# Regrouping TensorE's small-tile work, and a gate on VectorE, in a DiT block

## The chip, the cores and the metric

One core of one Trainium2 chip. The metric is the device time of one execution in microseconds (us). Whole times come from repeated executions; a profile is one execution. All whole times compared here are of runs recorded as fast.

Names: PE is TensorE's matmul stream, PEld its weight loads, DVE VectorE, ACT ScalarE, POOL GpSimd, SP SyncE, which starts the weight transfers. ACTq is ScalarE's instruction queue, here when it starts a transfer.

## The reference

A diffusion-transformer block, B = 2 batches of N = 256 tokens, D = 1152, F = 4608, H = 2 heads of Dh = 576.

```python
mod = (silu(c) @ w_mod).reshape(B, 6, 1, D)
shift_a, scale_a, gate_a, shift_m, scale_m, gate_m = [mod[:, i] for i in range(6)]
h = layernorm(x) * (1 + scale_a) + shift_a
q, k, v = split(h @ wqkv)                        # (B, N, H, Dh) each
attn = softmax(q @ k.T * Dh ** -0.5)             # per batch and head
x = x + gate_a * ((attn @ v) @ wo)
h2 = layernorm(x) * (1 + scale_m) + shift_m
return x + gate_m * (gelu(h2 @ w_fc1) @ w_fc2)
```

Dh = 576 is four and a half chunks of 128. The nine chunks of D are therefore four for head 0, one shared (64 rows to each head; `HC` = 4), and four for head 1. The shared chunk makes matmuls with half the rows in the scores, and with half the columns in the values.

## The kernel before

TensorE works through the block in order: k, q, then V with the scores between its groups, values, Wo, fc1, fc2. Four pairs of scores stand among the twelve V groups. Each ends in two matmuls on 64 rows:

```python
def score_pair(b, qt):
    ps = [acc_tile([P, N], "ps_s") for _ in range(H)]        # one PSUM bank each, six in rotation
    for h in range(H):
        for cc in whole:                                     # four chunks of 128 rows
            nc.tensor.matmul(ps[h][:], qT[:, cc, ...], kT[:, cc, ...], ...)
    for h in range(H):                                       # the shared chunk, 64 rows each
        nc.tensor.matmul(ps[h][:], qT[half(h), HC, ...], kT[half(h), HC, ...], ...)
    # ... negated maximum (DVE), exp with row sum (ACT); finish() divides (DVE)

SCORES_AT = {0: (0, 0), 1: (0, 1), 3: (1, 0), 4: (1, 1)}
TRANSPOSES_AT = {3: 0, 7: 1}                                 # two DMA transposes each, started by ACT
for i, (pnl, t) in enumerate(v_order):
    fin = score_pair(*SCORES_AT[i]) if i in SCORES_AT else None
    v_group(pnl, t)                                          # 9 matmuls of 384 columns, then an eviction
    # ... fin(), the transposes of attn
    if i == 8:
        shift_m = vec_section(sT, w_shift_m, "shift_m")      # 36 matmuls with 32 columns of weights
    if i == 10:
        scale_m = vec_section(sT, w_scale_m, "scale_m")
```

The values take the chunks of a batch in pairs, with the shared chunk (64 columns of weights) inside each batch. The MLP gate is a row vector made on TensorE within fc1: 36 matmuls with two columns of weights, four side by side in strips of 32 columns (`gate_natural`, called after m = 22). Its result goes through DRAM to be broadcast to all partitions. Evictions from PSUM, where this kernel's matmuls leave their sums, alternate between DVE and ACT. The code fixes the order in which each engine is given its instructions.

## Time and profile before

Three runs before the prediction: 247.61 us median (247.48 to 247.7).

```profile
span 245.6 us, 3980 instructions
PE 238.3 (97%) x1711; PEld 142.5 (58%) x1711; DVE 64.7 (26%) x175; ACT 63.3 (26%) x124; POOL 26.5 (11%) x39
```

TensorE is busy for 97% of the span (the busy table of the page), at a mean granted clock of 0.999. Its one hole after the start-up stands ahead of fc1's later chunks, in the timeline of PE (start, duration, what; in brackets the idle time before it and what ended it):

```profile
102.81 37.52 PE L639 MATMUL pacc<-hT,w_f 128*128 128x256 bf16 x265 [0.36 <-ACT hT L557]
```

So time is saved only by taking it out of TensorE's stream. What a piece of it costs is best read from the chain of work that ended last, as start to start: where PE is the limit its pieces follow one another, and the piece's second number is the time to the start of the next one. (start, us, what, count of matmuls.)

```profile
52.16 0.97 PE ps_s L456 x8
53.13 0.22 PE ps_s L461 x2
53.35 1.57 PE pacc L488 x9
54.92 0.87 PE ps_s L456 x8
...
62.79 7.42 PE pacc L488 x45
70.21 1.22 PE pn L375 x36
71.42 3.03 PE pacc L488 x18
74.45 1.22 PE pn L375 x36
...
77.24 0.87 PE pa L541 x8
78.11 0.34 PE pa L536 x4
78.45 1.85 PE pa L541 x16
...
81.62 4.40 PE pacc L589 x27
...
144.64 1.20 PE pg L408 x36
145.84 25.36 PE pacc L639 x117
171.20 70.30 PE pacc L693 x468
```

Here L488 is V, L456 and L461 the whole and half chunks of the scores, L375 the two modulation sections, L541 and L536 whole and half chunks of the values, L589 Wo, L408 the gate, L639 fc1, L693 fc2. A *visit* is here a stretch of matmuls of a smaller tile shape with full-size ones before and after it. Nine V matmuls right after a visit to half chunks take 1.57 us. Of the 45 in 7.42 us the first nine stand behind such a visit too; the other 36 take 7.42 - 1.57 = 5.85, or 1.46 for nine. The two 64-row matmuls start together (two records of 0.28 us each span 0.28 in the timeline of PE). By one whole matmul of the same 256 columns (0.87 / 8) they should stream in 0.11 us, an estimate; they take 0.21.

### The profile page before, as it was taken

How to read it: one execution, taken by the hardware profiler on the slowest of the kernel's cores; microseconds unless marked ns; L12 is line 12 of the kernel's file. 1: busy time of each engine (PE TensorE's matmuls, PEld its weight loads, DVE VectorE, ACT ScalarE, POOL GpSimd, SP SyncE). 2: the span in 40 equal slices, each digit the busy share in tenths (PEclk: the TensorE clock that was granted, in tenths of full speed). 3: DMA queues.
4: the chain of work that ended last, by engine and by line, in shares of the span. 5: the costliest groups of instructions: out<-in, count | busy, mean ns of one | idle time of the engine just before them, and what ended most of it. 6: DMA issues, size and time to landing. Idle time of an engine off the chain costs nothing.

```text
span 245.6 us, 3980 instructions
## 1 busy us (share of the span) xinstructions
PE 238.3 (97%) x1711; PEld 142.5 (58%) x1711; DVE 64.7 (26%) x175; ACT 63.3 (26%) x124; POOL 26.5 (11%) x39
## 2 busy tenths in 40 slices
PE   8799999999999999999999999999999999999993
PEld 2585444456656665788844444444566556666573
DVE  3752452226524499903000010000000000000001
ACT  7641350343312422670423332233000000000000
POOL 1000000031000234100000012100022111111111
PEclk9999999999999999999999999999999999999999
DMA  6999999999995999228999999991000000000000
GB/s 229 328 334 363 366 329 390 390 391 393 350 371 72 400 390 150 48 51 279 393 391 368 326 327 325 333 337 54 0 16 19 16 16 16 23 29 17 19 16 17
DMA packets 47373, 53.29 MB, mean 217 GB/s; under 512 B 8427, under 2 KB 34171, under 8 KB 47355
## 3 DMA queue, kind: packets, MB, share of 16 engines
q1 hardware_dynamic: 39840, 50.14, 60.7%
q10 hardware_dynamic: 6939, 1.71, 4.9%
q0 software_dynamic: 576, 1.19, 1.4%
q8 instruction: 13, 0.21, 0.4%
q14 instruction: 5, 0.04, 0.1%
HBM read 50.14 MB, written 1.19 MB: 209 GB/s over the span
## 4 chain that ended last, share of the span: by engine, by line
PE 86%; DVE 4%; DMA 4%; ACT 2%; issue 1%; ACTq 1%; SPq 0%; DVEq 0%
PE pacc L693 29%; PE pacc L639 27%; PE pacc L488 7%; PE pacc L430 7%; PE pk L263 4%; DMA w_scale_a<-in_w_mod_dram 3%; PE pk L292 2%; PE pacc L589 2%; PE pa L541 2%; PE pn L375 1%; PE ps_s L456 1%; DMA hT<-xn 1%; DVE stats L603 1%; DVE tmp L594 1%; PE pg L408 1%; ACT xn L579 1%
## 5 line engine op out<-in xcount | busy, mean ns | idle before, releaser
L639 PE MATMUL pacc<-hT,w_f 128*128 128x256 bf16 (+1 forms) x432 | 70.7, 326 | 0.4 <-ACT hT L557 0.4
L693 PE MATMUL pacc<-w_f,gT 128*128 128x384 bf16 (+2 forms) x468 | 70.5, 314 | 0.0
L693 PEld LDWEIGHTS <-gT 128*128 128x128 bf16 x468 | 44.3, 98 | 26.3
L639 PEld LDWEIGHTS <-w_f 128*128 128x128 bf16 x432 | 42.2, 98 | 28.4 <-issue 0.8
L699 DVE TENSOR_TENSOR tmp<-pacc,gate 128x384 f32<-128x384 f32 (+2 forms) x13 | 6.9, 527 | 88.2 <-PE pacc L693 88.2
L671 ACT ACTIVATE gT<-pacc 128x512 bf16<-128x512 f32 x24 | 14.3, 597 | 32.2 <-PE pacc L639 32.2
L701 POOL TENSOR_TENSOR o_sb<-tmp,x 128x384 bf16<-128x384 f32 (+1 forms) x12 | 11.7, 972 | 73.3 <-DVE tmp L699 73.3
L488 PE MATMUL pacc<-w_v,hT 128*128 128x384 bf16 x108 | 18.6, 327 | 0.0
L430 PE MATMUL pacc<-hT,w_q 128*128 128x512 bf16 x81 | 17.8, 380 | 0.0
L589 PE MATMUL pacc<-w_o,big 128*128 128x384 bf16 x108 | 17.7, 327 | 0.0
L589 PEld LDWEIGHTS <-big 128*128 128x128 bf16 x108 | 10.6, 98 | 6.9
L419 POOL DMA_DIRECT2D gates_dram<-nat x8 | 4.3, 544 | 93.2 <-DVE nat L416 93.2
L488 PEld LDWEIGHTS <-hT 128*128 128x128 bf16 x108 | 10.1, 98 | 7.2 <-issue 0.5
L263 PE MATMUL pk<-big,w_k 128*128 128x256 bf16 (+2 forms) x90 | 13.4, 294 | 0.4 <-ACT big L250 0.4
L430 PEld LDWEIGHTS <-w_q 128*128 128x128 bf16 x81 | 7.8, 98 | 9.6 <-issue 0.2
L416 DVE CAST nat<-pg 2x288 bf16<-2x288 f32 x4 | 1.8, 450 | 35.8 <-PE pg L408 35.7
L595 POOL TENSOR_TENSOR x<-tmp,x_sb 128x384 f32<-128x384 f32 x8 | 7.3, 911 | 36.3 <-DVE tmp L594 36.3
L263 PEld LDWEIGHTS <-w_k 128*128 128x128 bf16 x90 | 7.5, 97 | 3.4 <-DMA w_k<-in_wqkv_dram 0.3
L660 ACT ACTIVATE gT<-pacc 128x512 bf16<-128x512 f32 x12 | 6.5, 598 | 9.5 <-PE pacc L639 9.5
L156 PE MATMUL pwarm<-zeros 128*128 128x512 bf16 x19 | 7.2, 530 | 1.2 <-DVE eps_t L93 1.2
L594 DVE TENSOR_TENSOR tmp<-pacc,gate 128x384 f32<-128x384 f32 x12 | 6.6, 548 | 2.3 <-PE pacc L589 2.3
L250 ACT ACTIVATE big<-pt,scale_a 128x256 bf16<-128x256 bf16 (+1 forms) x12 | 4.6, 434 | 9.2 <-PE pt L241 7.4
(88 smaller groups left out, 146.7 us busy)
## 6 DMA issues: line engine op xcount, KB each, us to landing
w_f<-in_w_fc_dram SPq DMA_DIRECT2D x14, 864.0 KB, 10.5
w_f<-in_w_fc_dram SPq DMA_DIRECT2D x2, 2592.0 KB, 15.1
w_f<-in_w_fc_dram SPq DMA_DIRECT2D x2, 1728.0 KB, 12.0
w_shift_a<-in_w_mod_dram SPq DMA_DIRECT2D x3, 864.0 KB, 11.3
w_q<-in_wqkv_dram SPq DMA_DIRECT2D x3, 864.0 KB, 12.0
w_gate_a<-in_w_mod_dram SPq DMA_DIRECT2D x3, 864.0 KB, 10.1
w_v<-in_wqkv_dram SPq DMA_DIRECT2D x3, 864.0 KB, 13.3
w_shift_m<-in_w_mod_dram SPq DMA_DIRECT2D x3, 864.0 KB, 15.3
```

Source lines behind the costliest of these rows:

```text
L156: nc.tensor.matmul(dst[:], zeros[:, 0:P], zeros[:], start=True, stop=True)
L263: nc.tensor.matmul(pk[m][:, c0:c1], w_k[:, k, m * P:(m + 1) * P], hT0[:, k, c0:c1], start=(k == 0 and c0 == 0), stop=(k == KD - 1), skip_g ...
L430: nc.tensor.matmul(pacc[:], w_q[:, k, m * P:(m + 1) * P], hT[:, k, :], start=(k == 0), stop=(k == KD - 1),)
L488: nc.tensor.matmul(pacc[:], hT[:, k, t * P:(t + 1) * P], w_v[:, k, pnl * PW:(pnl + 1) * PW], start=(k == 0), stop=(k == KD - 1),)
L589: nc.tensor.matmul(pacc[:], aT[:, k, t * P:(t + 1) * P], w_o[:, k, c0:c1], start=(k == 0), stop=(k == KD - 1),)
L594: nc.vector.tensor_tensor(tmp[:], pacc[:], gate_a[:, b, c0:c1], op=ALU.mult)
L595: (nc.gpsimd if pool_add else nc.vector).tensor_tensor(x1[:, t, c0:c1], tmp[:], x_sb[:, t, c0:c1], op=ALU.add)
L639: nc.tensor.matmul(dst, w_f1[m // KD][:, k, ml * P:(ml + 1) * P], hT[:, k, c0:c1], start=start, stop=(k == KD - 1), **kw,)
L671: nc.scalar.activation(gT[:, m, :], pacc[:], ACT.Gelu_apprx_tanh)
L693: nc.tensor.matmul(pacc[:], gT[:, kk, t * P:(t + 1) * P], w_f2[j][:, r, c0 - n * PW:c0 - n * PW + cw], start=(kk == 0), stop=(kk == KF - 1),)
L699: nc.vector.tensor_tensor(tmp[:], pacc[:], gate_m[:, b, c0:c0 + cw], op=ALU.mult)
L701: (nc.vector if last else nc.gpsimd).tensor_tensor(o_sb[:], tmp[:], x1[:, t, c0:c0 + cw], op=ALU.add)
```

## The change

Four things, three of them meant to cut the number of times TensorE goes to a smaller tile shape and back:

1. Scores: all 40 matmuls in one block ahead of V, head 0's whole chunks first, and the eight half chunks in one run. Softmax then goes by batch and head, with one DVE instruction over 512 columns for the maxima of both row tiles, while V is computed.
2. Values: the half chunks of both batches in one run at the end.
3. `shift_m` and `scale_m` next to each other.
4. MLP gate on DVE: 18 passes over 128 x 1152, 32 x 32 transposes and reductions; only the sum over four groups of 32 partitions stays on TensorE, as two small fp32 matmuls near the end of fc1.

```diff
-    SCORES_AT = {0: (0, 0), 1: (0, 1), 3: (1, 0), 4: (1, 1)}
-    TRANSPOSES_AT = {3: 0, 7: 1}
+    for h in range(H):
+        whole = range(0, HC) if h == 0 else range(HC + 1, KD)
+        for b in range(B):
+            for qt in range(TPB):
+                for cc in whole:
+                    score_mm(b, h, qt, cc, slice(0, P), qt == 0 and cc == whole[0], False)
+    for b in range(B):
+        for qt in range(TPB):
+            for h in range(H):
+                score_mm(b, h, qt, HC, half(h), False, True)
...
     for i, (pnl, t) in enumerate(v_order):
+        if i < len(softmaxes):
+            softmaxes[i]()             # divides, then starts the DMA transpose of this (b, h)
         v_group(pnl, t)
-        if i == 8:
+        if i == 9:
             shift_m = vec_section(sT, w_shift_m, "shift_m")
-        if i == 10:
             scale_m = vec_section(sT, w_scale_m, "scale_m")
...
-    cpairs = [(0, 1), (2, 3), (4, 5), (6, 7), (8,)]
+    for b in range(B):
+        for chunks in ((0, 1), (2, 3), (5, 6), (7, 8)):
+            av = av_tile(chunks, b)
+    for b in range(B):
+        av_tile((HC,), b)
...
+    def gate_vector(g, wg):
+        for k in range(KD):
+            for b in range(B):
+                # k == 0: tensor_scalar_mul; else
+                nc.vector.scalar_tensor_tensor(
+                    part[:, b, :], wg[:, k, :], s32[:, k, b:b + 1], part[:, b, :],
+                    op0=ALU.mult, op1=ALU.add)
+        # six times: nc.vector.transpose of 384 columns, nc.vector.tensor_reduce over 32 -> folded
+    def gate_vector_finish(g, folded):
+        for b in range(B):
+            nc.tensor.matmul(pg[:, b, :], folded[:, b, :], fold[:], start=True, stop=True)
+        # ... cast, to DRAM, broadcast
...
         if m == 22:
-            gate_m = gate_natural(1, w_gate_m)
+            gate_m_finish = gate_vector(1, w_gate_m)
+        if m == KF - 2:
+            gate_m = gate_m_finish()
```

More of the change, by code (lines that the diff above doesn't have):

```diff
@@ L79, in wide_tile @@
         return wide.tile([P, KD, D], BF16, name=name, tag="wide")
-    x_sb = act.tile([P, NT, D], BF16, name="x_sb")
+    x_sb = act.tile([P, NT, D], BF16, name="x_sb", tag="x_sb")
     c_sb = act.tile([B * KD, P], BF16, name="c_sb")
@@ L399, with broadcast_gate @@
     k_evac(8)
+    s32 = const.tile([P, KD, B], FP32, name="s32")
+    nc.vector.tensor_copy(s32[:], sT[:, :, 0:B])
+    fold = const.tile([P, 32], FP32, name="fold")
+    nc.vector.tensor_reduce(fold[:], ident[:].rearrange("p (q a) -> p a q", a=32), axis=AX.X, op=ALU.add)
     gates_dram = tc.dram_tile([2, B, D], BF16, name="gates_dram")
+    def broadcast_gate(g):
+        gate = act.tile([P, B, D], BF16, name="gate", tag="gate")
+        for b in range(B):
+            nc.gpsimd.dma_start(gate[:, b, :], gates_dram[g, b:b + 1, :].partition_broadcast(P))
+        return gate
+    def gate_vector(g, wg):
+        part = act.tile([P, B, D], FP32, name="part", tag="x_sb")
+        folded = small.tile([P, B, D // 32], FP32, name="folded", tag="folded", bufs=1)
+        for k in range(KD):
+            for b in range(B):
+                if k == 0:
+                    nc.vector.tensor_scalar_mul(part[:, b, :], wg[:, k, :], s32[:, k, b:b + 1])
+                else:
+                    nc.vector.scalar_tensor_tensor(
+                        part[:, b, :], wg[:, k, :], s32[:, k, b:b + 1], part[:, b, :],
+                        op0=ALU.mult, op1=ALU.add,
+                    )
+        for b in range(B):
+            for c in range(0, D, PW):
+                blocks = work.tile([P, PW // 32, 32], FP32, name="tmp", tag="tmp", bufs=3)
+                nc.vector.transpose(blocks[:].rearrange("p j r -> p (j r)"), part[:, b, c:c + PW])
+                nc.vector.tensor_reduce(
+                    folded[:, b, c // 32:(c + PW) // 32], blocks[:], axis=AX.X, op=ALU.add
+                )
+        return lambda: gate_vector_finish(g, folded)
+    def gate_vector_finish(g, folded):
+        rows = D // 32
+        pg = aux_tile([rows, B, 32], "pg")
+        for b in range(B):
+            nc.tensor.matmul(pg[:, b, :], folded[:, b, :], fold[:], start=True, stop=True)
+        nat = work.tile([rows, B, 32], BF16, name="nat_v", tag="nat_v", bufs=1)
+        nc.vector.tensor_copy(nat[:], pg[:])
+        for b in range(B):
+            nc.gpsimd.dma_start(gates_dram[g, b, :].rearrange("(j r) -> j r", r=32), nat[:, b, :])
+        return broadcast_gate(g)
     def gate_natural(g, wg):
@@ L419, in gate_natural @@
             nc.gpsimd.dma_start(gates_dram[g, :, i * CTW:(i + 1) * CTW], nat[rows, :])
-        gate = act.tile([P, B, D], BF16, name="gate", tag="gate")
-        for b in range(B):
-            nc.gpsimd.dma_start(gate[:, b, :], gates_dram[g, b:b + 1, :].partition_broadcast(P))
-        return gate
+        return broadcast_gate(g)
     gate_a = None
@@ L448 @@
     attnT_all = soft[:, 3 * n_s * N:4 * n_s * N].rearrange("p (i n) -> p i n", n=2 * N)
-    def score_pair(b, qt):
-        q0 = b * N + qt * P
-        ps = [acc_tile([P, N], "ps_s") for _ in range(H)]
-        for h in range(H):
-            whole = range(0, HC) if h == 0 else range(HC + 1, KD)
-            for cc in whole:
-                nc.tensor.matmul(
-                    ps[h][:], qT[:, cc, q0:q0 + P], kT[:, cc, b * N:(b + 1) * N],
-                    start=(cc == whole[0]), stop=False,
-                )
-        for h in range(H):
-            nc.tensor.matmul(
-                ps[h][:], qT[half(h), HC, q0:q0 + P], kT[half(h), HC, b * N:(b + 1) * N],
-                start=False, stop=True,
-            )
-        parts = []
-        for h in range(H):
-            negmax = small.tile([P, 1], FP32, name="negmax", tag="negmax")
-            nc.vector.reduce_max(negmax[:], ps[h][:], axis=AX.X, negate=True)
-            si = (b * H + h) * TPB + qt
-            rowsum = small.tile([P, 1], FP32, name="rowsum", tag="rowsum")
-            nc.scalar.activation(
-                e_all[:, si, :], ps[h][:], ACT.Exp, bias=negmax[:], scale=1.0, accum_out=rowsum[:]
-            )
-            parts.append((si, rowsum))
-        def finish():
-            for si, rowsum in parts:
-                rs = small.tile([P, 1], FP32, name="rs", tag="rs")
-                nc.vector.reciprocal(rs[:], rowsum[:])
-                nc.vector.tensor_scalar_mul(attn_all[:, si, :], e_all[:, si, :], rs[:])
@@ new lines, in attn_transpose, with score_mm @@
+    def attn_transpose(i):
+        pair = attn_all[:, TPB * i:TPB * (i + 1), :].rearrange("p i n -> p (i n)")
+        nc.scalar.dma_start_transpose(attnT_all[:, i, :].rearrange("p (c n) -> p c n", n=P), pair)
+    ps = {(b, h): acc_tile([P, TPB, N], "ps_s") for b in range(B) for h in range(H)}
+    def score_mm(b, h, qt, cc, rows, first, last):
+        q0 = b * N + qt * P
+        nc.tensor.matmul(
+            ps[(b, h)][:, qt, :], qT[rows, cc, q0:q0 + P], kT[rows, cc, b * N:(b + 1) * N],
+            start=first, stop=last, skip_group_check=True,
+        )
@@ new lines, with softmax, finish @@
+    for h in range(H):
[4 more added lines that the diff above has]
+                    score_mm(b, h, qt, cc, slice(0, P), qt == 0 and cc == whole[0], False)
+    for b in range(B):
+        for qt in range(TPB):
+            for h in range(H):
+                score_mm(b, h, qt, HC, half(h), False, True)
+    def softmax(b, h):
+        i = b * H + h
+        negmax = small.tile([P, TPB], FP32, name="negmax", tag="negmax")
+        rowsum = small.tile([P, TPB], FP32, name="rowsum", tag="rowsum")
+        nc.vector.tensor_reduce(negmax[:], ps[(b, h)][:], axis=AX.X, op=ALU.max, negate=True)
+        for qt in range(TPB):
+            nc.scalar.activation(
+                e_all[:, i * TPB + qt, :], ps[(b, h)][:, qt, :], ACT.Exp,
+                bias=negmax[:, qt:qt + 1], scale=1.0, accum_out=rowsum[:, qt:qt + 1],
+            )
+        def finish():
+            rs = small.tile([P, TPB], FP32, name="rs", tag="rs")
+            nc.vector.reciprocal(rs[:], rowsum[:])
+            for qt in range(TPB):
+                nc.vector.tensor_scalar_mul(
+                    attn_all[:, i * TPB + qt, :], e_all[:, i * TPB + qt, :], rs[:, qt:qt + 1]
+                )
+            attn_transpose(i)
@@ L492, in v_group @@
         evac(v_sb[:, t, pnl * PW:(pnl + 1) * PW], pacc[:])
-    def attn_transpose(i):
-        pair = attn_all[:, TPB * i:TPB * (i + 1), :].rearrange("p i n -> p (i n)")
-        nc.scalar.dma_start_transpose(attnT_all[:, i, :].rearrange("p (c n) -> p c n", n=P), pair)
-    SCORES_AT = {0: (0, 0), 1: (0, 1), 3: (1, 0), 4: (1, 1)}
-    TRANSPOSES_AT = {3: 0, 7: 1}
     v_order = [(pnl, t) for pnl in range(NPD) for t in range(NT)]
-    shift_m = scale_m = None
+    softmaxes = [softmax(b, h) for b in range(B) for h in range(H)]
     for i, (pnl, t) in enumerate(v_order):
-        fin = score_pair(*SCORES_AT[i]) if i in SCORES_AT else None
+        if i < len(softmaxes):
+            softmaxes[i]()
         v_group(pnl, t)
-        if fin is not None:
-            fin()
-        if i in TRANSPOSES_AT:
-            for h in range(H):
-                attn_transpose(TRANSPOSES_AT[i] * H + h)
-        if i == 8:
+        if i == 9:
             shift_m = vec_section(sT, w_shift_m, "shift_m")
-        if i == 10:
             scale_m = vec_section(sT, w_scale_m, "scale_m")
@@ L524, in attnT, with av_tile @@
         return blocks[:, kc, :, :]
-    cpairs = [(0, 1), (2, 3), (4, 5), (6, 7), (8,)]
-    for b in range(B):
-        for cp in cpairs:
-            pa = acc_tile([P, len(cp), N], "pa")
-            for ci, cc in enumerate(cp):
-                dst = pa[:, ci, :].rearrange("p (q n) -> p q n", n=P)
-                for kc in range(TPB):
-                    vt = v_sb[:, b * TPB + kc, cc * P:(cc + 1) * P]
-                    if cc == HC:
-                        for h in range(H):
-                            nc.tensor.matmul(
-                                dst[half(h), :, :], vt[:, half(h)], attnT(b, h, kc),
-                                start=(kc == 0), stop=(kc == TPB - 1),
-                            )
-                    else:
-                        av = nc.tensor.matmul(
-                            dst, vt, attnT(b, cc // (HC + 1), kc),
-                            start=(kc == 0), stop=(kc == TPB - 1),
-                        )
-            if b == 0 and cp == cpairs[0]:
+    def av_tile(chunks, b):
+        pa = acc_tile([P, len(chunks), N], "pa")
+        for ci, cc in enumerate(chunks):
+            for kc in range(TPB):
+                vt = v_sb[:, b * TPB + kc, cc * P:(cc + 1) * P]
+                dst = pa[:, ci, :].rearrange("p (q n) -> p q n", n=P)
+                for h in (range(H) if cc == HC else [cc // HC]):
+                    rows = half(h) if cc == HC else slice(0, P)
+                    av = nc.tensor.matmul(
+                        dst[rows, :, :], vt[:, rows], attnT(b, min(h, H - 1), kc),
+                        start=(kc == 0), stop=(kc == TPB - 1),
+                    )
+        evac(aT[:, chunks[0]:chunks[-1] + 1, b * N:(b + 1) * N], pa[:])
+        return av
+    for b in range(B):
+        for chunks in ((0, 1), (2, 3), (5, 6), (7, 8)):
+            av = av_tile(chunks, b)
+            if b == 0 and chunks[0] == 0:
                 tc.add_manual_dep(first_load["w_f1_0"], av.ins.name, WAIT_FOR, reason="transposes first")
-            evac(aT[:, cp[0]:cp[0] + len(cp), b * N:(b + 1) * N], pa[:])
+    for b in range(B):
+        av_tile((HC,), b)
     x1 = act.tile([P, NT, D], FP32, name="x1", tag="x1")
```

## The prediction

> **What bounds the kernel.** TensorE: the busy table gives PE 238.3 of 245.6 us (97%), the chain of waits is 86% PE. The only PE hole after the start-up is 0.36 us at 102.8 us (ScalarE, hT), just before fc1. Only time taken out of the PE stream counts.
>
> **What the change removes.** The chain of waits gives start-to-start times. Nine 384-column matmuls of V take 1.47 us (five groups in 7.42), but 1.57 after a visit with 64-row, 64-column or 32-column tiles: leaving such a visit costs about 0.10 us, entering it about the same (two 64-row score halves, which start together, take 0.21; two 64-column pairs of values 0.34, against 0.22 of streaming). [...]
> - Scores: four visits become one. Now 0.97 + 3x0.87 + 4x0.21 + 4x0.10 = 4.8 us; after, 32 full matmuls at 0.109, four concurrent pairs at 0.11 and two switches: 4.15. Saves 0.65.
> - Values: two visits become one: saves 0.22.
> - Shift_m and scale_m together: one entry and one exit go: saves 0.22.
> - MLP gate: 1.20 us of matmuls at 144.64 and an exit of 0.11 go: saves 1.3.
>
> **What it adds.** On PE two fp32 36x32 matmuls near the end of fc1[...]. On VectorE 18 passes over 128x1152: by this trace's fp32 tensor-tensor (384 columns: 0.55 us alone, 0.46 apart) about 1.3 us each, plus six transposes and reductions, about 1 us a pair: 29 to 31 us. w_gate_m lands at 130.7 to 135 us, VectorE is idle from there to 171, so it ends near 161, 5 us before PE reaches the two matmuls at about 166.5.
>
> **Critical path.** All PE savings lie on it. Slack checked: softmax keeps four PSUM banks of six; by the measured reductions and Exp the first is free about 58 us, and V's third group asks near 59. V's eighth group waits for an eviction behind two transpose issues (1.3 us each) on ScalarE, margin 3 us. Transposes land by 75, values start near 76. Scale_m lands near 67, used at 72. The gate arrives at 172 to 180; five free banks of 5.9 us each cover that. One fc2 load now waits for VectorE (w_gate_m's slot, 153 us), needed at 195.
>
> **Prediction.** 0.65 + 0.22 + 0.22 + 1.3[...] = 1.95 us: 245.6 us (0.8% faster); 8 in 10 between 244.9 and 246.6. Faster by over 2%: 0.01; within 2%: 0.95; slower: 0.04.
>
> **What would show it.** Windows: about 4.1 us from the first score matmul to the first of V, PE without a hole; one visit of about 2.4 us for both sections; values 4.2 us (now 4.38); no PE visit near 144; VectorE's gate block of about 30 us ending before 165; two short PE matmuls near 166[...]; the LN2 hole of about 0.4 us kept.
>
> **What would make it wrong.** VectorE passes at half the rate (2.6 us each): the block ends after 180, and PE stands still for over 10 us. PSUM waits in V (PE holes at 59 to 70 us) if the softmax queues up. Score halves that don't pair: +0.4. fp32 matmuls dearer than estimated.

Passages are cut from this text where marked, because no trace or run showed what they said or rested on: one on what happens in TensorE at a change of shape, and the figures for the two fp32 matmuls, made before any trace held one. The forecast's sum came to 1.95 us. The four savings still in it come to 2.39; the term cut was subtracted, and was the author's estimate of what those two matmuls cost.

## The result

The changed kernel takes 245.31 us median of four runs (245.19 to 245.86), beside 247.55 for the kernel before. The ratio is 0.9914 (95% interval 0.9896 to 0.9931). A ratio here is the mean time of one kernel's fast runs over that of the other's of the same rounds, so it is not quite the ratio of the medians quoted. The change saves about 2.1 us, or 0.9%; 245.6 had been predicted. The interval leaves out 1.

The profiled run of the changed kernel happened to be the slowest of the four (245.86); a second profile, taken later, has a span of 243.4 us. Nearly all of this difference lies before the first score matmul: that starts at 53.10 us in one and at 52.44 in the other (52.16 in the kernel before). The stages behind it agree to 0.02 us. This is why stages are compared below, and not spans.

```profile
span 244.1 us, 3930 instructions
PE 237.0 (97%) x1679; PEld 142.6 (58%) x1679; DVE 91.7 (38%) x198; ACT 62.1 (25%) x122; POOL 25.4 (10%) x37
```

TensorE has 32 matmul records fewer (1711 to 1679), DVE 27 us more work. The chain, for the same stages as before:

```profile
53.10 4.04 PE ps_s L501 x40
57.13 14.73 PE pacc L543 x90
71.86 2.32 PE pn L375 x72
74.18 3.03 PE pacc L543 x18
77.21 4.05 PE pa L577 x40
81.26 4.51 PE pacc L632 x27
...
167.69 0.26 PE pg L442 x4
167.95 2.05 PE pacc L682 x9
170.00 70.30 PE pacc L738 x468
```

The reader should see one piece where there were many: scores 4.04 us, V in one run, both sections in one visit of 2.32 us, values 4.05 us, and the gate's 1.20 us turned into 0.26. The first piece after such a visit still pays: Wo's 27 matmuls take 4.51 us where they took 4.40, and nine fc1 matmuls 2.05 where q's, of the same width, take 1.94 (63 in 13.60 us in the kernel before).

The gate on DVE, in DVE's timeline:

```profile
130.06 1.55 DVE L422 TENSOR_SCALAR part<-w_gate_m,s 128x1152 f32<-128x1152 bf16 x2 [17.62 <-DMA w_gate_m<-in_w_mod_dram]
131.52 21.35 DVE L424 SCALAR_TENSOR_TENSOR part<-w_gate_m,s,part 128x1152 f32<-128x1152 bf16 x16
...
158.76 0.55 DVE L432 TENSOR_REDUCE folded<-tmp 128x12 f32<-128x384 f32 x1
167.99 0.22 DVE L444 CAST nat_v<-pg 36x64 bf16<-36x64 f32 x1 [8.68 <-PE pg L442]
```

It runs from 130.06 to 159.3 us, 29.3 us, and then DVE waits 8.68 us for TensorE: it is off the path, with about 8 us to spare.

### The profile page after: what moved, and what is told of

Same layout as the page of the kernel before. It is cut to its first block, busy times and chain, and to the rows that moved or that the text cites. A ratio compares the mean times of both kernels' runs of the same rounds, so it can differ in the third digit from the quotient of the medians.

```text
span 244.1 us, 3930 instructions
## 1 busy us (share of the span) xinstructions
PE 237.0 (97%) x1679; PEld 142.6 (58%) x1679; DVE 91.7 (38%) x198; ACT 62.1 (25%) x122; POOL 25.4 (10%) x37
## 4 chain that ended last, share of the span: by engine, by line
PE 89%; DVE 4%; DMA 2%; ACT 2%; ACTq 1%; issue 1%; DVEq 0%
PE pacc L738 29%; PE pacc L682 28%; PE pacc L543 7%; PE pacc L472 7%; PE pk L263 4%; PE pk L292 2%; PE pwarm L156 2%; PE pacc L632 2%; PE pa L577 2%; PE ps_s L501 2%; PE pn L375 1%; DMA hT<-xn 1%; DVE stats L646 1%; DMA c_sb<-in_c_dram 1%; DVE tmp L637 1%; ACT xn L622 1%
## 5 line engine op out<-in xcount | busy, mean ns | idle before, releaser
L424 DVE SCALAR_TENSOR_TENSOR part<-w_gate_m,s,part 128x1152 f32<-128x1152 bf16 x16 | 21.3, 1413 | 0.0
L543 PE MATMUL pacc<-w_v,hT 128*128 128x384 bf16 x108 | 17.9, 326 | 0.0
L746 POOL TENSOR_TENSOR o_sb<-tmp,x 128x384 bf16<-128x384 f32 (+1 forms) x12 | 11.6, 970 | 54.4 <-DVE tmp L744 54.4
L156 PE MATMUL pwarm<-zeros 128*128 128x512 bf16 x19 | 8.0, 580 | 1.2 <-DVE eps_t L93 1.2
L422 DVE TENSOR_SCALAR part<-w_gate_m,s 128x1152 f32<-128x1152 bf16 x2 | 1.6, 818 | 17.6 <-DMA w_gate_m<-in_w_mod_dram 17.6
L446 POOL DMA_DIRECT2D gates_dram<-nat_v x2 | 1.1, 531 | 68.0 <-DVE nat_v L444 68.0
```

Of the source, the lines that this page charges most:

```text
L156: nc.tensor.matmul(dst[:], zeros[:, 0:P], zeros[:], start=True, stop=True)
L424: nc.vector.scalar_tensor_tensor(part[:, b, :], wg[:, k, :], s32[:, k, b:b + 1], part[:, b, :], op0=ALU.mult, op1=ALU.add,)
L543: nc.tensor.matmul(pacc[:], hT[:, k, t * P:(t + 1) * P], w_v[:, k, pnl * PW:(pnl + 1) * PW], start=(k == 0), stop=(k == KD - 1),)
L746: (nc.vector if last else nc.gpsimd).tensor_tensor(o_sb[:], tmp[:], x1[:, t, c0:c0 + cw], op=ALU.add)
```

## The experiments

Theory: each visit of TensorE to another tile shape costs about 0.2 us beyond the streaming of its columns, and what the change saves is three visits in the scores, one in the values, one in the sections, and the gate's matmuls. First rival: the gate alone carries the gain, the regrouping gains nothing. Second rival, for the scores: they gain by not interrupting V and not waiting for q's last eviction, not by fewer visits.

The stages are read from the chain of each run: A, first score matmul to first values matmul; B, from there to fc1's restart after its hole; C, from there to the first fc2 matmul. All in us, as differences of starts.

| kernel | A | B | C | ratio to before (interval) |
|---|---|---|---|---|
| before | 25.08 | 25.57 | 68.39 | |
| changed | 24.11 | 25.34 | 67.45 | 0.9914 (0.9896 to 0.9931) |
| changed, again | 24.12 | 25.34 | 67.45 | 0.9911 (0.9898 to 0.9924) |
| before + scores | **24.34** | 25.58 | 68.40 | 0.9979 (0.9967 to 0.9991) |
| before + values | 25.07 | **25.36** | 68.40 | 0.9998 (0.9985 to 1.0011) |
| before + sections | **24.85** | 25.60 | 68.39 | 1.0003 (0.9987 to 1.0018) |
| before + gate | 25.07 | 25.57 | **67.45** | 0.9956 (0.9944 to 0.9968) |
| changed, scores in 4 visits | **24.76** | 25.34 | 67.45 | 0.9932 (0.992 to 0.9945) |
| changed, values in 4 visits | 24.12 | **26.01** | 67.45 | 0.9937 (0.9925 to 0.995) |
| changed, gate ends on DVE | 24.11 | 25.36 | **67.08** | 0.9894 (0.988 to 0.9907) |

fc2 takes 70.30 or 70.31 us in every run of the table.

### One part at a time

Each kernel is the one before with one part of the change (diffs as above). All gave correct results.

> Kernel before plus only the scores part: all 40 score matmuls in one block ahead of V, the 64-row halves in one run. Theory (each visit of TensorE to another tile shape costs about 0.2 us[...], so three visits fewer, plus 0.1 us of waiting for the last q eviction): from the first score matmul to the first values matmul 25.1 us becomes 24.4, whole time -0.65 us (ratio 0.9974). Rival (nearly all of the gain of the change is the gate's matmuls, taken off TensorE; regrouping gains nothing): 25.1 us stays, ratio 1.000.

> Kernel before plus only the values part: the two visits of 64-column halves become one at the end. Theory: from the first values matmul to the first fc1 matmul 0.22 us less (ratio 0.9991, at the edge of what whole times show, so read from the trace). Rival: nothing (ratio 1.000).

> Kernel before plus only shift_m and scale_m in one visit. Theory: from the first score matmul to the first values matmul 25.1 us becomes 24.9 (0.22 us less, ratio 0.9991). Rival: nothing (ratio 1.000).

> Kernel before plus only the MLP gate on VectorE. Theory: fc1, from the matmul after the ScalarE hole to the first fc2 matmul, 68.4 us becomes 67.45 (1.31 us of gate visit go, 0.37 us of two short fp32 matmuls come), whole time -0.94 us (ratio 0.9962). Rival (regrouping gains nothing, so the gate carries all 2.1 us): -2.1 us (ratio 0.9914).

Measured, from the table: scores -0.74 us in A, values -0.21 in B, sections -0.23 in A, gate -0.94 in C. Each moves its own stage and no other by more than 0.03 us. They sum to 2.12 us; the whole change takes 0.97 + 0.23 + 0.94 = 2.14 out of the three stages. So the parts add, and the first rival falls: the gate carries less than half.

Two of the four could not be told from nothing by the whole time: values and sections came out at 0.9998 and 1.0003, where 0.9991 was expected. Both intervals contain the expected value and 1 as well. One source of the scatter is visible, in one profile of each kernel: the first score matmul started anywhere between 52.16 and 52.74 us in these five profiles, ahead of all that was changed. The stages show what the clock on the whole cannot.

### Visits put back: scores

```diff
                 for cc in whole:
                     score_mm(b, h, qt, cc, slice(0, P), qt == 0 and cc == whole[0], False)
-    for b in range(B):
-        for qt in range(TPB):
-            for h in range(H):
-                score_mm(b, h, qt, HC, half(h), False, True)
+                if h == H - 1:
+                    for hh in range(H):
+                        score_mm(b, hh, qt, HC, half(hh), False, True)
```

> Changed kernel, scores still in one block ahead of V and softmax unchanged, but each of the four pairs of 64-row halves directly behind its own whole chunks: four visits in place of one. Theory (visits): the block, first score matmul to first V matmul, 4.04 us becomes 4.6 (three visits at 0.2), ratio to the kernel before about 0.9938 in place of 0.9914. Rival (the scores' gain came from taking softmax out of the V groups and not waiting for the q eviction, not from visits): 4.04 us stays.

The same 40 matmuls, the same softmax and the same V; only the half chunks stand in four visits. The chain:

```profile
52.56 4.67 PE ps_s L501 x40
57.24 14.73 PE pacc L542 x90
```

The block takes 4.67 where it took 4.04. Three visits more cost 0.63 us, 0.21 each (0.64 in A, of the second profile). The second rival falls for this part. What remains of the scores' 0.74 us, 0.10, fits the first pair of scores before (0.97 where later ones take 0.87), which is where a wait for q's last eviction would show (PEld's timeline has 0.20 us of it there, at 52.85 us).

### Visits put back: values

```diff
+    def hc_pair(pa, b, kc):            # the two half-chunk matmuls of one kc
+        ...
     for b in range(B):
-        for chunks in ((0, 1), (2, 3), (5, 6), (7, 8)):
+        pa_hc = acc_tile([P, N], "pa")
+        for ti, chunks in enumerate(((0, 1), (2, 3), (5, 6), (7, 8))):
             av = av_tile(chunks, b)
-    for b in range(B):
-        av_tile((HC,), b)
+            if ti in (1, 2):
+                hc_pair(pa_hc, b, ti - 1)
+            if ti == 2:
+                evac(aT[:, HC, b * N:(b + 1) * N], pa_hc[:])
```

> Changed kernel, but the values' 64-column halves in four visits (one after the second and one after the third tile of each batch) in place of one. The kernel before had two. Theory: first values matmul to first fc1 matmul grows by three visits, about 0.6 us; first values matmul to first Wo matmul 4.05 becomes about 4.6. Rival (a switch is hidden behind the weight loads): no change.

```profile
76.80 0.87 PE pa L577 x8
77.67 0.23 PE pa L586 x2
77.90 0.54 PE pa L577 x4
78.44 0.23 PE pa L586 x2
```

A pair of 64-column matmuls takes 0.23 us, and the four whole ones after it 0.54 where four stream in 0.44 (half of the 0.87 for eight). B grows from 25.34 to 26.01: 0.67 us for three visits, 0.22 each. One visit (25.34), two (25.57, the kernel before) and four (26.01) lie on a line. So the cost is per visit, not per matmul, and it is not hidden. One size was missed: to the first Wo matmul it takes 4.83 us (76.80 to 81.63), not the expected 4.6, because the last visit is now left within the values and no longer at Wo (whose 27 matmuls take 4.40 again, in place of 4.51).

### The gate made late

```diff
+        junk = small.tile([P, 1], FP32, name="junk", tag="junk", bufs=1)
+        for _ in range(12):
+            nc.vector.tensor_reduce(junk[:], part[:, 0, :], axis=AX.X, op=ALU.add)
         for b in range(B):
             for c in range(0, D, PW):
```

> Changed kernel with 12 extra reductions over 1152 columns on VectorE ahead of the gate's transposes[...]. Theory (the gate on VectorE is free as long as it ends before TensorE asks, with 8.3 us of slack; after that TensorE stands still one for one): a TensorE hole of about 7 us before the two fp32 matmuls, and the time 6 to 7.5 us longer than that of the changed kernel. Rival (TensorE passes over the waiting matmuls, or the later stages absorb it): no hole, same time.

The time was 254.65 us, ratio 1.0273: some 9 us more than the changed kernel, not 6 to 7.5. The hole is there. PE's timeline:

```profile
159.79 7.29 PE L685 MATMUL pacc<-hT,w_f 128*128 128x512 bf16 x32
172.06 0.33 PE L445 MATMUL pg<-fold,folded 128*36 128x32 f32 x2 [4.99 <-DVE folded L435]
175.28 0.33 PE L445 MATMUL pg<-fold,folded 128*36 128x32 f32 x2 [2.89 <-DVE folded L435]
175.54 3.53 PE L685 MATMUL pacc<-hT,w_f 128*128 128x512 bf16 x9
```

C grew from 67.45 to 77.13, 9.68 us, from two terms. The twelve reductions took 16.6 us (1.38 each), and 16.6 less the 8.3 of slack is 8.3 us of waiting. That is more than the 7 expected, which rested on the estimate of the reductions; no run had shown one of that size. And the nine fc1 matmuls after it took 3.46 us start to start in place of 2.05, 1.4 us more, because TensorE's clock had dropped. In the windows view of this run, each line one stretch, the clock is the number behind the POOL entry:

```profile
170.00:175.00 5.00, 0.33 (x2) 0.20 (x2) 4.83 (x10) 0.00 (x0) 0.00 (x0) 0.66 0.01 4
176.00:177.00 1.00, 1.00 (x4) 0.39 (x3) 0.00 (x0) 0.00 (x0) 0.84 (x2) 0.50 0.00 0
```

The reading fell to 0.50 within the hole of 4.99 us, about 4.5 us after its start. That is an estimate: the mean of 0.66 from 170 to 175 us puts the fall at 171.6, if the reading went from 1.00 to 0.50 in one step, and the last matmul before the hole ended at 167.08. So the theory holds (free while early, one for one when late), with a surcharge that I had not counted.

### The last step of the gate moved off TensorE

```diff
-        for b in range(B):
-            nc.tensor.matmul(pg[:, b, :], folded[:, b, :], fold[:], start=True, stop=True)
+        for q in range(3):
+            nc.vector.tensor_copy(moved[q][:], folded[32 * (q + 1):32 * (q + 2)])
+        # three additions of 32 x 72, the last into a bf16 tile padded to 128 columns,
+        # one 32 x 32 transpose; four DMAs to DRAM in place of two
```

> Changed kernel with the last step of the gate (the sum over the four groups of 32 partitions) on VectorE too: no TensorE visit is left in fc1. Theory: the fp32 visit costs 0.26 us plus 0.11 us on leaving, so fc1 67.45 us becomes 67.1, ratio to the kernel before about 0.990. Rival (the fp32 visit is hidden, its 0.26 us are pipeline latency): fc1 stays 67.45.

The median was 245.06 us (244.85 to 245.34), beside 247.78 for the kernel before. C is 67.08, 0.37 less than in the changed kernel: 0.26 of visit and 0.11 of exit, as expected, so the fp32 visit was not hidden. The kernel before is 0.23 higher in this call than in the last one below, so this run is compared with the changed kernel by the stage, not by the median.

### Three follow-ups, and a stage that ran out of slack

The last four runs share their rounds. The changed kernel came out at 245.33 us (245.22 to 245.48), the kernel before at 247.55.

> The changed kernel once more, for the same chip and rounds as the three below. Ratio to the kernel before 0.9914 as recorded, windows as in its first profile: 24.1 us first score to first values matmul, 67.45 us in fc1.

It repeated to 0.01 us per stage (table).

> Changed kernel with one step moved on ScalarE: the modulation of chunk 5 (first batch) goes ahead of the normalization of the third row tile, in place of behind its transpose issue. Theory: the one TensorE hole, 0.36 us ahead of chunk 5 in fc1, is an order on ScalarE and goes; the third tile's transpose is issued 0.5 us later, which the second batch has room for (its modulations start at 110.0 us, TensorE asks near 111). Time -0.3 to -0.4 us against the changed kernel. Rival (the chain through the vector engines is the limit, so the hole only moves to the second batch): same time, a hole near 111 us.

```diff
-    BETWEEN = {2: ((0, "d"), (1, "d"), (2, "a"), (3, "a")), 3: ((8, "d"),)}
+    BETWEEN = {2: ((0, "d"), (1, "d"), (2, "a"), (3, "a"), (5, "a")), 3: ((8, "d"),)}
...
-            ln2_modulate(0, 5, "a")
```

244.8 us (244.74 to 244.91, no overlap with the changed kernel's range), ratio to before 0.989. The hole is gone: from the start of Wo at 80.69 the chain now runs through TensorE alone.

```profile
80.69 17.66 PE pacc L632 x108
98.34 68.26 PE pacc L681 x423
166.60 0.26 PE pg L442 x4
```

From the first values matmul to the first fc2 matmul it takes 92.26 us where the changed kernel takes 92.79, 0.53 less. That is more than the 0.36 us that the timeline showed as idle, and more than was expected. The records have the difference: one of these 256-column matmuls is shown as 0.27 us long, while they follow one another at 0.11 (155 in 17.08 us). The last 0.16 us of a record are thus covered by the next matmul where there is one, and an idle time counted from a record's end is that much too short: 0.36 + 0.16 = 0.52. The rival falls: no hole came up in the second batch.

> Changed kernel with the attention gate's TensorE visit moved from between two q groups to just ahead of the score halves, so that two visits of other tile shapes stand side by side. Theory (each change of shape costs about 0.1 us): four changes become three, 0.1 us less from the first q matmul to the first V matmul (23.0 to 22.9). Rival (a change between two small shapes costs as much as two with the full shape): no difference.

```diff
-        if m == 6:
-            gate_a = gate_natural(0, w_gate_a)
...
+    gate_a = gate_natural(0, w_gate_a)
     for b in range(B):
         for qt in range(TPB):
             for h in range(H):
                 score_mm(b, h, qt, HC, half(h), False, True)
```

> All three of the follow-ups on the changed kernel: the gate's last step on VectorE, chunk 5 ahead on ScalarE, the attention gate beside the score halves. If they add up, -0.37 -0.36 -0.1 = -0.83 us against the changed kernel, about 244.5 us, ratio to the kernel before 0.988.

Both missed, and in the same way. The attention gate beside the score halves: 247.82 us (ratio 1.0019, interval 1.0002 to 1.0036). All three together: 247.46 (ratio 1.002, 0.9982 to 1.0058), where 0.988 was expected. The term that I had counted seems to have come: from the first q matmul to the first V matmul four profiles of kernels with the changed kernel's code up to there show 22.82 or 22.83 us, and the two with the gate moved 22.73 and 22.72, 0.1 less as the theory says. (Two more, the changed kernel's first profile among them, show 23.00, with 0.17 more in q that the record doesn't explain.) But a hole came up in V. The profile with the attention gate moved alone was recorded as slow, so the lines are those of the kernel with all three (fast). ACT's timeline:

```profile
62.83 8.66 ACTq L496 DMA_TRANSPOSE soft<-soft  x2
71.54 1.24 ACT L275 CAST big<-pacc 128x384 bf16<-128x384 f32 x3 [8.31 <-issue]
```

and PE's:

```profile
72.07 1.62 PE L545 MATMUL pacc<-w_v,hT 128*128 128x384 bf16 x9 [2.35 <-ACT big L275]
```

The tenth V group uses the PSUM bank of the fourth (four of six banks went to the scores, then the rotation goes on). ACT evicts the fourth, but only after it has started the last two DMA transposes of the attention weights, and starting them held its queue for 8.66 us. TensorE stood still for 2.35 us until that eviction was done, and from the first V matmul to the first values matmul it took 22.60 us where the changed kernel takes 20.08: 2.52 more, again 0.17 above the idle time shown.

The slow profile of the other kernel shows a longer hole, and what came with it. PE's timeline, and a line of the windows view:

```profile
73.28 3.04 PE L542 MATMUL pacc<-w_v,hT 128*128 128x384 bf16 x9 [3.51 <-ACT big L275]
74.00:76.00 2.00, 2.00 (x8) 0.76 (x6) 0.00 (x0) 0.00 (x0) 0.00 (x0) 0.50 1.22 229
```

Its hole in V is 3.51 us, and within it the clock fell to 0.50 for 6.8 us, as after the late gate; from 80 us on it reads 1.00. The fall came about 2.4 us after the last matmul before the hole (at 72.12, by the same estimate from a mean of 0.53 over 72 to 74 us), sooner than the 4.5 us of the late gate, while the hole of 2.35 us in the kernel with all three left the reading at 1.00. The cause of the difference is open. So this profile is slow for a wait of its own, as far as its trace shows. Both kernels scatter widely (246.95 to 250.47 for the one with all three, whose interval is therefore wide); whether the same lies behind their other long runs, the record can't tell, since they have no profile.

The same order exists in the changed kernel, where it was only not late. Its ACT timeline, and that of the kernel before:

```profile
61.55 1.24 ACTq L495 DMA_TRANSPOSE soft<-soft  x1
62.83 0.48 ACT L275 CAST big<-pacc 128x384 bf16<-128x384 f32 x1 [1.40 <-DVE rs L530]
62.91 6.21 ACTq L495 DMA_TRANSPOSE soft<-soft  x2
69.16 1.24 ACT L275 CAST big<-pacc 128x384 bf16<-128x384 f32 x3 [5.86 <-PE pacc L543]
```

```profile
61.74 2.96 ACTq L497 DMA_TRANSPOSE soft<-soft  x2
68.84 2.54 ACTq L497 DMA_TRANSPOSE soft<-soft  x2
```

The bracket of the last line of the first fence names PE, but the fourth group was done at about 63.1 us (57.13 + 1.57 + 3 x 1.46); it was ACT's own queue that was late. The fourth group's eviction ends at 69.16 + 0.48 = 69.64 us, and the tenth group starts at 57.13 + 1.57 + 8 x 1.46 = 70.38. The margin is 0.7 us. In every run with the regrouped scores and the attention gate in its old place (eight profiles) the last two starts took 6.2 to 6.3 us; in the two with the gate moved, 9.8 (the slow profile) and 8.7. Why they take longer there was not isolated. What lies next to them is the broadcast of the attention gate out of DRAM: it is started at 63.7 us in the kernel with all three and at 56.8 in the changed one. That it is the cause is an argument, not a result.

So no single run combines the two gains without this loss. In the kernel with all three, the stretch behind V, from the first values matmul to the first fc2 matmul, takes 91.91 us against the changed kernel's 92.79: 0.88 less, which is nearly the 0.53 and 0.37 together. The two without the attention gate's move would be worth about 244.4 us, an estimate by that sum (245.33 - 0.90); such a kernel was not run. The best one that ran is the changed kernel with chunk 5 moved, 244.8 us; by its ratio, 0.989, it can't be told from the one whose gate ends on DVE (0.9894).

## Why the prediction was right

- **The bound.** TensorE's stream; whatever left it came off the time: 2.14 us in the stages, about 2.1 in the whole time (1.95 predicted).
- **A visit costs 0.2 us.** Right, and it holds with visits taken away and put back: 0.21 and 0.22 each, about half of it on each side (an exit 0.11, from 1.57 less 1.46 for nine V matmuls). What takes the time was not shown: PEld stands idle for 0.21 us before the first load of the new shape, at 56.52 and 57.06 us in the changed kernel, but no run tests whether that is the cause.
- **Scores.** 0.65 predicted, 0.74 measured. The block takes 4.04 us where 4.15 was predicted. **Values and sections** 0.22 each predicted, 0.21 and 0.23 measured.
- **Gate on TensorE.** 1.3 us of matmuls and exit predicted to go, less an estimate for the two fp32 matmuls; net 0.94 measured. The fp32 part was the term that was put too dear: it took 0.37 us (0.26 and an exit of 0.11). The trace records two matmul instructions for each fp32 one (four for two, in the chain).
- **Gate on VectorE.** 29 to 31 us predicted, 29.3 measured; a pass of 1152 columns lasts 1.41 us, and the passes are 1.33 us apart. The slack, put at 5 us, was 8.3. The broadcast gate was predicted for 172 to 180 us; the first multiplication with it starts at 176.1, and five free banks covered the wait (fc2's matmuls show no idle time).
- **What was seen too kindly.** The prediction gave the ScalarE evictions behind the transposes a margin of 3 us, for V's eighth group, at 1.3 us per transpose start. For the eighth group that is about right (its bank is free at 63.3, it starts at 67.5). The tight one is the tenth group, which I had not checked, and the third and fourth transpose start take 2.7 and 3.5 us, not the 1.26 and 1.24 of the first two, when all four follow one another. The real margin was 0.7 us. That it held was luck as far as the prediction goes; the follow-up that fell over it shows what it was worth. The transposes were also later than predicted: not landed by 75, but at about 76.7 and 77.3 for the third and fourth (started at 62.9 and 65.7, 13.8 and 11.6 us to landing). It cost nothing either, since the second batch's values, which read these two, start at about 79 us.

## What to carry to other kernels

Where TensorE is the limit, count how often it goes to another tile shape and back: each round trip cost 0.2 us here, for three kinds of small tiles, so gather such work into one visit, or give it to an engine that stands idle. Read gains of this size from start-to-start times of a stage, since the start-up alone moved by up to 0.9 us from profile to profile. And after a regrouping, go through every bank of the rotation for the eviction that frees it, not only the nearest one: here the queue that started four DMA transposes in a row was held for 6.2 to 8.7 us by the last two, and the evictions behind them were late.
